# Reciprocal sums broadcast through a DRAM scratch, TensorE's steps from a table, border splits on VectorE

## The chip, the cores and the metric

One core of a Trainium2 chip runs one program in one launch. Time is in device microseconds. A core has TensorE (matmuls; PE in the profile, and PEld for its weight loads), VectorE (DVE), ScalarE (ACT), GpSimd (POOL), SyncE (SP, which here only issues transfers), and 16 DMA engines between DRAM and the on-chip memory. Each engine works through its own instructions in the order in which they were written for it; semaphores hold an instruction until what it needs is there.

## The reference, cut to what matters

Attention with a threshold, then two feed-forward layers. Scores that lie more than `tau` under their row's maximum are masked out; what is left is exponentiated and divided by its row sum.

```python
scores = (1 / np.sqrt(64)) * np.matmul(q, k.transpose(0, 1, 3, 2))   # 4 x 8 heads, 576 x 576
thresh = np.max(scores, axis=-1, keepdims=True) - tau
scores = np.where(scores >= thresh, scores, -1e9)
attn = np.exp(scores - np.max(scores, axis=-1, keepdims=True))
attn = attn / (np.sum(attn, axis=-1, keepdims=True) + 1e-09)
x = np.matmul(attn, v)                       # then to 2304 tokens x 512
h = x @ w_in                                 # 512 x 2048
x = (np.maximum(h, 0) + alpha * np.minimum(h, 0)) @ w_out
h = x @ w2_in
return (h * (1 / (1 + np.exp(-h)))) @ w2_out
```

## The kernel before

**Attention stage.** The 32 heads are worked in 16 pairs (`pairs`). A pair has nine units `t`: units 0 to 7 are 128 rows of queries of one head (even units the first head, odd ones the second), and unit 8 holds the last 64 rows of both heads. The steps of a unit, with the engine and the line of the profile:

- TensorE, `qkmm` (L345): scores of two units into PSUM, tile `s`.
- VectorE, `maxi` (L359): scales and negates the scores into a buffer `x` and takes the row's extreme.
- ScalarE, `expo` (L372) and `thr` (L379): the exponentials, tile `e` (unit 8: `z`), and the threshold.
- VectorE, `mask` (L385): multiplies the exponentials by the comparison with the threshold and takes the row sum into column 2 of `stat(i)`, tile `m`.
- TensorE, `trans` (L420): transposes the masked exponentials in pieces of 128 x 128 into a PSUM bank, tile `t`; ScalarE copies a bank into on-chip memory (`copy`, L130, tiles `pt`, `p`, `px`, `q`).
- TensorE, `pv` (L454, five steps per pair) and `pv8` (L461, unit 8): the product with the values.
- VectorE, `evac` (L468) and `evac8` (L475): bring the product into `X`, multiplied by the reciprocal of the row sum.

That product has queries along the free dimension, while the row sums stand one to a partition, so the reciprocals have to be turned. Before, this went by way of TensorE: `recip` (L394, three times per pair: four, four and one column), `spread` (L400, on ScalarE: each column copied 64 times into a tile `rb`), `transr` (L426: five more transposes per pair, into the same PSUM banks as transposes of the last key block), and the copies of those banks, which are twice as wide for it. `evac` and `evac8` then read the turned reciprocals from `px` and `q`.

**What sets the order.** TensorE's steps were one cycle, `CYCLE`, repeated for every pair with offsets (`Q2:-1` is the scores of unit 2 of the pair before). `plan` places every other engine's instructions: at each moment an engine takes, of what is ready by the planner's own durations, that with the lowest priority number. Idle TensorE time early on is filled with dummy matmuls on a zero tile (`idle`, L288: `WU` = 9 before all else, `WF` = 32 more where the planner sees a gap). The order so found is written out and kept by the engines. SyncE's queue holds the loads of `raw` (queries and keys), `rv` (values) and `wraw` (weights), in that order too.

**Weights and border.** The feed-forward layers take their weights split into a high and a low part (`wconv`, L164 to L180: about ten instructions per 128 x 512 piece, on ScalarE, VectorE and, after the attention stage, GpSimd: L176, L178). The eight pieces of the first quarter of the first layer are made during the attention stage, at low priority. The first product of the first layer, `mm_h` (L209), for tokens 0 to 511 is 48 matmuls into tiles `s`; `act1` (L218, L219) applies the activation and `hilo` (L130, L126) splits the result `g` into a high part (ScalarE) and a low part (VectorE); `ymm` (L625, L641) multiplies by the second weights, tile `y`. `xsplit` (L197) does the same splitting for `X`, with the low part on GpSimd (L126 on POOL, tile `xs`). From there on the layers are one long row of `h` and `y` matmuls. "The border" below is the stretch in which the attention stage ends and this row begins.

Of the kernel before, what the change touches and what calls it, by code (L numbers as in the profile page):

```python
# [36 lines left out]
WF = 32  # L37
# [8 lines left out]
CYCLE = (  # L46
# [56 lines left out]
def attn_moe_moe(  # L103
# [139 lines left out]
    with ExitStack() as pa:  # L243
# [7 lines left out]
        rbp = ent(name="rbp", bufs=2)  # L251
# [137 lines left out]
        def cols(ch):  # L389
            return (0, 1) if ch == 2 else (4 * ch + 1, 4 * ch + 5)  # L390

        def recip(i, ch):
            a, z = cols(ch)
            V.reciprocal(stat(i)[:, 2, a:z], stat(i)[:, 2, a:z])  # L394

        def spread(i, ch):
            a, z = cols(ch)
            n = 2 if ch == 2 else 4
            RS[i, ch] = rbp.tile([128, 4, 64], F32, tag="rb", name="rb")
            A.activation(out=RS[i, ch][:, :n], in_=stat(i)[:, 2, a:z].unsqueeze(2).to_broadcast([128, n, 64]), func=AF.Copy)  # L400

        cycle = [(x.split(":")[0], int(x.split(":")[1])) for x in CYCLE.split()]
        line = [(x, i + o) for i in range(0, NP + 2) for x, o in cycle if 0 <= i + o < NP]
# [45 lines left out]
        def pv(i, kt):  # L449
            if kt == 0:  # L450
                AV[i] = psV.tile([128, 512], F32, tag="pv", name="pv")
            for h in range(2):
                src = PT[i, "pt"][:, h, kt] if kt < KT - 1 else PT[i, "px"][:, 0]
                T.matmul(AV[i][h * 64:(h + 1) * 64], RV[i][:, h, kt], src, start=kt == 0, stop=kt == KT - 1)  # L454

        def pv8(i):
# [263 lines left out]
```

## Time and profile before

| what | value |
|---|---|
| median of 3 runs | 1078.13 us (1077.79 to 1078.48) |
| the profiled execution: time, span | 1078.86 us, 1077.1 us |
| mean granted TensorE clock | 0.997 |
| busy in the span: PE, PEld, DVE, ACT, POOL | 1067.9, 835.3, 745.3, 606.3, 357.4 us |
| attention stage (to the first of the 48 `h` matmuls) | 0 to 279.5 us |
| the 48 `h` matmuls, then the first 24 `y` matmuls | 279.5 to 290.6, to 296.2 us |
| TensorE idle, then at half clock | 296.2 to 298.8, about 300.0 to 303.4 us |
| rest of the layers | to 1077.1 us |

Busy time is the share of time in which an engine has an instruction in work; where one starts before the last has ended (VectorE's do), starts give the real spacing. In the chain of waits each moment belongs to the instruction that held up the end. A matmul's end is modelled, so the spacing of starts is used for TensorE too. The profiled execution's span is 1.76 us shorter than its time, and its time is 0.73 us above the median of the runs.

### The profile page before, as it was taken

The numbers are of one execution on the slowest core, as the hardware profiler recorded it, in microseconds if no ns is written. First come the engines' busy times: TensorE is split into PE (matmuls) and PEld (weight loads), VectorE is DVE, ScalarE is ACT, GpSimd is POOL, SyncE is SP. The second block draws the span as 40 slices with busy tenths as digits, with TensorE's granted clock in tenths as the row PEclk, the third lists the DMA queues.
The fourth block names the chain that finished last, engine by engine and source line by source line (L and its number), as shares of the span: only waits on it lengthen the run. The fifth ranks groups of instructions, "written<-read, shape, count | busy, mean of one in ns | idle before, by whom it ended". The sixth has DMA issues, their size and how long they took to land.

```text
span 1077.1 us, 15422 instructions
## 1 busy us (share of the span) xinstructions
PE 1067.9 (99%) x5749; PEld 835.3 (78%) x5749; DVE 745.3 (69%) x1403; ACT 606.3 (56%) x1177; POOL 357.4 (33%) x271
## 2 busy tenths in 40 slices
PE   9999999999999999999999999999999999999998
PEld 5656666566678888888888888888888888888887
DVE  7999999999766278558846864863478468543343
ACT  5898898888665455345534543565455354433321
POOL 0000000000355285256625742851566256323110
PEclk9999999999999999999999999999999999999999
DMA  3223232221222011101201110121012011000112
GB/s 107 74 92 96 70 104 66 81 84 39 79 79 79 1 59 59 40 19 60 79 1 40 59 59 1 59 64 35 19 61 79 1 40 59 1 1 1 40 59 79
DMA packets 19402, 57.09 MB, mean 53 GB/s; under 512 B 2432, under 2 KB 2816, under 8 KB 19328
## 3 DMA queue, kind: packets, MB, share of 16 engines
q1 hardware_dynamic: 18880, 55.71, 16.2%
q8 instruction: 45, 0.74, 0.3%
q10 hardware_dynamic: 448, 0.41, 0.1%
q14 instruction: 29, 0.24, 0.1%
HBM read 51.39 MB, written 4.72 MB: 52 GB/s over the span
## 4 chain that ended last, share of the span: by engine, by line
PE 94%; DVE 3%; ACT 1%; issue 1%; DMA 0%; POOL 0%; DVEq 0%; ACTq 0%; SPq 0%
PE h L209 36%; PE y L641 18%; PE y L625 18%; PE s L345 8%; PE t L420 6%; PE pv L454 6%; DVE x L359 1%; PE pv L288 1%; DVE e L385 1%; PE t L461 1%; PE t L426 1%; DMA wraw<-in_w1i 0%; ACT pt L130 0%; DVE wa L168 0%; DVE wm L166 0%
## 5 line engine op out<-in xcount | busy, mean ns | idle before, releaser
L209 PE MATMUL h<-xs,w 128*128 128x512 f32 (+1 forms) x1872 | 418.7, 368 | 0.0
L209 PEld LDWEIGHTS h<-xs,w 128*128 128x128 f32 x1872 | 329.8, 189 | 60.1
L176 POOL TENSOR_TENSOR wa<-wa,w 128x512 f32<-128x512 f32 x56 | 72.9, 1302 | 458.8 <-ACT w L172 359.9
L625 PE MATMUL y<-g,w 128*128 128x512 f32 (+1 forms) x960 | 216.9, 370 | 2.7 <-ACT g L130 2.7
L641 PE MATMUL y<-w,g 128*128 128x512 f32 x876 | 213.9, 387 | 0.0
L625 PEld LDWEIGHTS y<-g,w 128*128 128x128 f32 x960 | 169.9, 189 | 34.1 <-ACT g L130 3.1
L641 PEld LDWEIGHTS y<-w,g 128*128 128x128 f32 x876 | 161.4, 188 | 32.0
L126 DVE TENSOR_TENSOR g<-r,g 128x512 fp32r<-128x512 f32 (+1 forms) x160 | 140.0, 875 | 56.3 <-ACT g L130 54.9
L126 POOL TENSOR_TENSOR xs<-acc,xs 128x512 fp32r<-128x512 f32 (+1 forms) x80 | 106.0, 1355 | 133.5 <-ACT xs L130 133.4
L130 ACT ACTIVATE g<-r 128x512 fp32r<-128x512 f32 (+1 forms) x160 | 93.9, 587 | 92.5 <-DVE r L229 47.1
L126 POOL TENSOR_TENSOR xs<-X,xs 128x512 fp32r<-128x512 f32 (+1 forms) x72 | 98.7, 1399 | 57.5 <-ACT xs L130 57.1
L359 DVE TENSOR_SCALAR_CACHE_REDUCE x<-s,nsc 128x576 f32<-128x576 f32 x144 | 112.4, 814 | 7.1 <-PE s L345 6.1
L229 DVE TENSOR_TENSOR r<-h,r 128x512 f32<-128x512 f32 (+1 forms) x80 | 50.7, 634 | 92.7 <-ACT r L228 92.4
L219 DVE SCALAR_TENSOR_TENSOR r<-r,neg,h 128x512 f32<-128x512 f32 (+1 forms) x76 | 52.2, 686 | 73.8 <-ACT r L218 73.6
L345 PE MATMUL s<-raw 64*128 64x288 f32 (+1 forms) x576 | 100.6, 429 | 0.9 <-DVE x L359 0.9
L228 ACT ACTIVATE r<-h 128x512 f32<-128x512 f32 (+1 forms) x80 | 43.8, 547 | 102.2 <-PE h L209 101.7
L372 ACT ACTIVATE e<-x,m 128x576 f32<-128x576 f32 x128 | 97.0, 790 | 7.4 <-DVE x L359 7.4
L385 DVE SCALAR_TENSOR_TENSOR e<-x,m,e 128x577 f32<-128x577 f32 x128 | 99.7, 811 | 1.2 <-ACT m L379 1.0
L180 DVE TENSOR_TENSOR w<-we,wa 128x512 fp32r<-128x512 f32 x64 | 59.9, 935 | 46.1 <-POOL we L178 33.8
L345 PEld LDWEIGHTS s<-raw 64*128 64x128 f32 (+1 forms) x576 | 57.2, 188 | 40.8 <-DVE e L385 11.4
L172 ACT ACTIVATE w<-wa 128x512 fp32r<-128x512 f32 x64 | 40.7, 635 | 84.4 <-DVE wa L168 77.5
L178 POOL TENSOR_TENSOR we<-we,wm 128x512 f32<-128x512 f32 x56 | 81.6, 1457 | 18.2 <-ACT wm L174 18.2
(69 smaller groups left out, 1043.3 us busy)
## 6 DMA issues: line engine op xcount, KB each, us to landing
wraw<-in_w1i SPq DMA_DIRECT2D x16, 512.0 KB, 3.8
wraw<-in_w1o SPq DMA_DIRECT2D x16, 512.0 KB, 3.5
wraw<-in_w2i SPq DMA_DIRECT2D x16, 512.0 KB, 3.6
wraw<-in_w2o SPq DMA_DIRECT2D x16, 512.0 KB, 3.4
rv<-in_v SPq DMA_DIRECT2D x16, 480.0 KB, 3.5
raw<-in_q SPq DMA_DIRECT2D x15, 320.0 KB, 3.3
out<-o SPq DMA_DIRECT2D x17, 256.0 KB, 2.0
raw<-in_k SPq DMA_DIRECT2D x15, 288.0 KB, 2.8
```

Of the source, the lines that this page charges most:

```text
L126: le.tensor_tensor(out=lo, in0=src, in1=hi.bitcast(F32), op=ALU.subtract)
L130: e.activation(out=dst, in_=src, func=AF.Copy)
L176: e2.tensor_tensor(out=a, in0=a, in1=w[:, 0].bitcast(F32), op=ALU.subtract)
L178: e2.tensor_tensor(out=e, in0=e, in1=m, op=ALU.mult)
L209: nc.tensor.matmul(ps[:, :n], w[c][:, a, fl * 128:(fl + 1) * 128], xs[c][:, b, :n], start=k == 0, stop=k == 3 * NC - 1,)
L345: T.matmul(SP[u + k][:, hf, :S // 2], RAW[i][p, 0, q], RAW[i][p, 1, c], start=True, stop=True)
L359: V.tensor_scalar(out=x.rearrange("p (a b) -> p a b", a=2), in0=SP[u][:, :, :S // 2], scalar1=nsc, scalar2=None, op0=ALU.mult, op1=ALU.min ...
L372: A.activation(out=ES[u], in_=xts[u % XB][:, 1:S + 1], func=AF.Exp, bias=mcol(u, 0), scale=-1.0)
L385: V.scalar_tensor_tensor(out=e, in0=x, scalar=mcol(u, 1), in1=e, op0=ALU.is_le, op1=ALU.mult, accum_out=mcol(u, 2))
L420: T.transpose(TP[n][:, c * 128:(c + 1) * 128], EP[i, t // 2][:, o:o + 128], ident)
L625: nc.tensor.matmul(ys[e][:, :n], w[NC + fl][:, a, e * 128:(e + 1) * 128], gt[:, c, :n], start=fl == 0 and k == 0, stop=fl == G - 1 and k == 2,
L641: nc.tensor.matmul(y, gt[:, a, s * 128:(s + 1) * 128], w[NC + fl][:, c, cs], start=fl == 0 and k == 0, stop=fl == G - 1 and k == 2,)
```

## The change

- The reciprocals are taken once per pair, nine columns at a time (`recip`), then written to a DRAM scratch by one transfer that turns them (`keep`: 1152 elements of 4 bytes), and read back by four transfers that repeat them over 64 partitions each (`fetch`), into a tile `inv` in the layout that `evac` and `evac8` multiply by. `spread` and `transr` and their shares of the copies are gone; `evac8` is one instruction instead of two.
- TensorE's steps come from a table, `ORDER`, that gives each step of each pair its place, and priorities by kind (`PRIO`) replace those in the calls. `WF` goes from 32 to 16, and the first `pv` waits for the last filler.
- The first two weight pieces of the second quarter, and the split of `X` for tokens 1024 to 1535, have their low parts made by VectorE instead of GpSimd.

```diff
-WF = 32
+WF = 16
-CYCLE = (
-    "Q2:-1 T6:-2 T2:-2 T7:-2 T0:-2 Tr1:-2 Q4:-1 T8:-2 Rr1:-2 "
...
+ORDER = (
+    "Q0:0 Q2:0 T1:0 Q4:0 Q6:0 Tr0:0 T0:0 T3:0 Q8:0 T4:0 T2:0 Q0:1 T6:0 T7:0 T5:0 Q2:1 P0:0 Tr1:0 Q4:1 T8:0 T0:1 "
...
+PRIO = {'exp': 2, 'copy': -1, 'thr': 0.5, 'mask': 2.5, 'max': 0, 'recip': 2.5, 'evac': 0, 'evac8': 0, 'w': 2.5, 'xh': 2.5, 'xl': 2.5}
...
-            it = wconv(stage, pools[j // NC], wi, wo, g, j, nc.gpsimd)
+            it = wconv(stage, pools[j // NC], wi, wo, g, j, V if wi is w1i and g == 1 and j < 2 else nc.gpsimd)
...
-        def recip(i, ch):
-            a, z = cols(ch)
-            V.reciprocal(stat(i)[:, 2, a:z], stat(i)[:, 2, a:z])
-
-        def spread(i, ch):
...
+        def recip(i):
+            V.reciprocal(stat(i)[:, 2], stat(i)[:, 2])
+
+        def keep(i):
+            SC[i] = dram.tile([9, 128], F32, tag="inv", name="inv")
+            nc.sync.dma_start(SC[i].rearrange("t q -> q t"), stat(i)[:, 2])
+
+        def fetch(i):
+            RS[i] = ptp.tile([128, S], F32, tag="inv", name="inv")
+            for h in range(2):
+                src = SC[i][1:].rearrange("(j h) q -> h j q", h=2)[h].unsqueeze(0).to_broadcast([64, 4, 128])
+                nc.sync.dma_start(RS[i][h * 64:(h + 1) * 64, :512].rearrange("p (j q) -> p j q", q=128), src)
+            for h in range(2):
+                src = SC[i][0:1, h * 64:(h + 1) * 64].to_broadcast([64, 64])
+                nc.sync.dma_start(RS[i][h * 64:(h + 1) * 64, 512:], src)
...
-        def transr(n):
...
-            V.tensor_tensor(out=X[:, hp, b * S:b * S + 512], in0=AV[i], in1=PT[i, "px"][:, 1], op=ALU.mult)
+            V.tensor_tensor(out=X[:, hp, b * S:b * S + 512], in0=AV[i], in1=RS[i][:, :512], op=ALU.mult)
...
-            for h in range(2):
-                p = slice(h * 64, (h + 1) * 64)
-                V.tensor_tensor(
-                    out=X[p, hp, c0:c0 + 64], in0=TP[bank[i, "r8"]][p, 256:320],
-                    in1=PT[i, "q8"][p, 128 + h * 64:192 + h * 64], op=ALU.mult,
-                )
+            V.tensor_tensor(
+                out=X[:, hp, c0:c0 + 64], in0=TP[bank[i, "r8"]][:, 128:192], in1=RS[i][:, 512:], op=ALU.mult
+            )
...
+                op(("recip", i), "DVE", 0.16, 0, [("mask", pos[i, x]) for x in range(9)], lambda i=i: recip(i), 0.3)
+                op(("keep", i), "SP", 0.6, 1, [("recip", i), ("fetch", i - 2)], lambda i=i: keep(i), 5.0)
+                op(("fetch", i), "SP", 2.4, 1, [("keep", i), ("evac", i - 2), ("evac8", i - 2)], lambda i=i: fetch(i), 4.5)
...
-                xs = xsplit(X[:, :, t0:t0 + n] if m == 1 else ACC[t0 // 512], n, nc.scalar, nc.gpsimd)
+                le = V if (m, g, t0) == (1, 0, 1024) else nc.gpsimd
+                xs = xsplit(X[:, :, t0:t0 + n] if m == 1 else ACC[t0 // 512], n, nc.scalar, le)
```

TensorE, in the middle of the attention stage; `t<-ident` are transposes, of which those that read `rb` are the turned reciprocals. Before:

```order
L345 MATMUL s<-raw 128x288 x4
L420 MATMUL t<-ident,e 128x128 x12
L345 MATMUL s<-raw 128x288 x2
L420 MATMUL t<-ident,z 128x128
L420 MATMUL t<-ident,e 128x128 x6
L426 MATMUL t<-ident,rb 128x128 x3
L345 MATMUL s<-raw 128x288 x4
L454 MATMUL pv<-pt,rv 64x512 x2
```

and in the changed kernel:

```order
L464 MATMUL pv<-pt,rv 64x512 x6
L363 MATMUL s<-raw 128x288 x4
L436 MATMUL t<-ident,e 128x128 x2
L436 MATMUL t<-ident,z 128x128 x4
L436 MATMUL t<-ident,e 128x128 x8
L363 MATMUL s<-raw 128x288 x2
L436 MATMUL t<-ident,e 128x128 x4
L436 MATMUL t<-ident,z 128x128
```

The transposes of `rb` are gone, and the blocks between the score groups are mixed otherwise. Counting every change between scores, transposes and `pv` work as one, TensorE's row has 150 blocks before and 160 now (fillers and the first `h` matmuls counted with the transposes). Twelve of the 48 `h` matmuls now stand ahead of the last pair's `pv` steps; before, all 48 stood behind them. Of the sixteen fillers all now stand ahead of the fourth group of scores of the first pair.

SyncE's queue, a stretch in the middle of the attention stage. Before:

```order
L316 DMA raw_1869<-in_q 128x640
L332 DMA rv_1929<-in_v 128x960
L316 DMA raw_2045<-in_k 128x576
L316 DMA raw_2045<-in_q 128x640
L332 DMA rv_2113<-in_v 128x960
L158 DMA wraw_2123<-in_w1o 128x1024
L316 DMA raw_2235<-in_k 128x576
```

and now (`inv<-m` is `keep`, `inv<-inv` is `fetch`):

```order
L334 DMA raw_1772<-in_k 128x576
L334 DMA raw_1772<-in_q 128x640
L412 DMA inv_1829<-m_1634 128x9x1
L350 DMA rv_1832<-in_v 128x960
L418 DMA inv_1882<-inv_1829 64x4x128 x2
L421 DMA inv_1882<-inv_1829 64x64 x2
L176 DMA wraw_1907<-in_w1o 128x1024
L334 DMA raw_1949<-in_k 128x576
L334 DMA raw_1949<-in_q 128x640
```

Five issues per pair join the queue; for the last pair a `wraw` load stands between `keep` and `fetch`. On VectorE, between a pair's reciprocal and the first instruction that reads its `inv`, stand 17 to 24 other instructions for pairs 0 to 14, and 13 for the last.

VectorE at the border, from the first activation of the first layer on (`r`, then `g`; `wm`, `wa`, `we`, `w` belong to weight pieces). Before:

```order
L219 SCALAR_TENSOR_TENSOR r_3173<-r_3173,neg_76,s_3075 128x512
L126 TENSOR_TENSOR g_3174<-r_3173,g_3174 128x512
L219 SCALAR_TENSOR_TENSOR r_3179<-r_3179,neg_76,s_3075 128x512
L180 TENSOR_TENSOR w_3214<-we_3213,wa_3212 128x512
L126 TENSOR_TENSOR g_3180<-r_3179,g_3180 128x512
L166 TENSOR_SCALAR wm_3226<-wm_3226 128x512
L168 SCALAR_TENSOR_TENSOR wa_3227<-wraw_3224,wm_3226 128x512
L170 TENSOR_SCALAR we_3228<-wa_3227 128x512
L219 SCALAR_TENSOR_TENSOR r_3185<-r_3185,neg_76,s_3108 128x512
L126 TENSOR_TENSOR g_3186<-r_3185,g_3186 128x512
L219 SCALAR_TENSOR_TENSOR r_3191<-r_3191,neg_76,s_3108 128x512
L126 TENSOR_TENSOR g_3192<-r_3191,g_3192 128x512
```

and now:

```order
L237 SCALAR_TENSOR_TENSOR r_3044<-r_3044,neg_76,s_2803 128x512
L198 TENSOR_TENSOR w_2940<-we_2939,wa_2938 128x512
L144 TENSOR_TENSOR g_3045<-r_3044,g_3045 128x512
L237 SCALAR_TENSOR_TENSOR r_3050<-r_3050,neg_76,s_2803 128x512
L144 TENSOR_TENSOR xs_3336<-X_81,xs_3336 128x512
L144 TENSOR_TENSOR g_3051<-r_3050,g_3051 128x512
L144 TENSOR_TENSOR xs_3339<-X_81,xs_3339 128x512
L144 TENSOR_TENSOR xs_3342<-X_81,xs_3342 128x512
L184 TENSOR_SCALAR wm_3082<-wm_3082 128x512
L237 SCALAR_TENSOR_TENSOR r_3056<-r_3056,neg_76,s_2974 128x512
L186 SCALAR_TENSOR_TENSOR wa_3083<-wraw_3080,wm_3082 128x512
L144 TENSOR_TENSOR xs_3345<-X_81,xs_3345 128x512
```

The four `xs` splits and, further on, `wa` and `we` of two weight pieces come into VectorE's row and leave GpSimd's.

## Rows read from the trace of the kernel before

**Rows 1.** The page's first part: busy time, share of the span and number of instructions of each engine.

```profile
PE 1067.9 (99%) x5749; PEld 835.3 (78%) x5749; DVE 745.3 (69%) x1403; ACT 606.3 (56%) x1177; POOL 357.4 (33%) x271
```

**Rows 2.** Busy time of each engine in stretches of the run: from and to (us), length, then busy time and number of instructions of PE, PEld, DVE, ACT and POOL, the granted TensorE clock (1.00 is 2.4 GHz, 0.50 is 1.2 GHz), the DMA engines' share and GB/s.

```profile
28.85:176.63 147.78, 147.78 (x1101) 92.43 (x1102) 144.77 (x405) 130.21 (x275) 0.00 (x0) 1.00 0.28 87
176.63:211.16 34.53, 33.89 (x247) 21.10 (x248) 34.24 (x95) 31.23 (x67) 0.00 (x0) 1.00 0.27 81
...
290.55:296.20 5.65, 5.60 (x25) 4.32 (x23) 5.62 (x4) 2.57 (x5) 5.57 (x4) 1.00 0.04 14
296.20:298.80 2.60, 0.00 (x0) 0.00 (x1) 1.87 (x4) 1.80 (x4) 1.25 (x2) 1.00 0.00 0
298.80:303.11 4.31, 4.31 (x13) 3.38 (x13) 3.58 (x6) 1.64 (x3) 1.94 (x2) 0.64 0.40 122
...
320.00:1077.10 757.10, 752.92 (x3600) 634.38 (x3598) 452.30 (x625) 344.24 (x637) 335.37 (x250) 1.00 0.13 42
```

**Rows 3.** The chain of waits in order of time: start, length, what.

```profile
61.80 2.73 PE pv L454 x12
...
78.19 2.73 PE pv L454 x12
...
176.63 2.73 PE pv L454 x12
...
183.83 1.47 DVE e L385 x3
...
211.16 2.73 PE pv L454 x12
...
311.62 2.72 PE y L625 x12
```

**Rows 4.** Timeline of TensorE in the middle of the attention stage, transposes of `rb` only: start, length, engine, line, what.

```profile
227.29 0.38 PE L426 MATMUL t<-ident,rb 128*128 128x128 f32 x2
...
234.66 0.49 PE L426 MATMUL t<-ident,rb 128*128 128x128 f32 x3
```

**Rows 5.** Groups of instructions by line over the attention stage: busy time in us, mean ns of one, then idle time of the engine before them.

```profile
L426 PE MATMUL t<-ident,rb 128*128 128x128 f32 x80 | 14.1, 273 | 0.0
...
L394 DVE RECIPROCAL m<-m 128x4 f32<-128x4 f32 (+1 forms) x48 | 8.0, 166 | 0.0
L475 DVE TENSOR_TENSOR X<-t,q 64x64 f32<-64x64 f32 x32 | 6.8, 212 | 0.7 <-PE t L461 0.5
```

**Rows 6.** Timeline of VectorE around the end of a pair: start, length, engine, line, what.

```profile
236.35 0.82 DVE L359 TENSOR_SCALAR_CACHE_REDUCE x<-s,nsc 128x576 f32<-128x576 f32 x1
...
237.09 0.82 DVE L359 TENSOR_SCALAR_CACHE_REDUCE x<-s,nsc 128x576 f32<-128x576 f32 x1
...
237.83 0.18 DVE L394 RECIPROCAL m<-m 128x4 f32<-128x4 f32 x1
237.92 0.79 DVE L385 SCALAR_TENSOR_TENSOR z<-x,m,z 128x577 f32<-128x577 f32 x1
...
238.64 0.45 DVE L475 TENSOR_TENSOR X<-t,q 64x64 f32<-64x64 f32 x2
...
239.12 0.69 DVE L468 TENSOR_TENSOR X<-pv,px 128x512 f32<-128x512 f32 x1
239.73 0.15 DVE L394 RECIPROCAL m<-m 128x1 f32<-128x1 f32 x1
239.80 0.80 DVE L385 SCALAR_TENSOR_TENSOR e<-x,m,e 128x577 f32<-128x577 f32 x1
```

**Rows 7.** Timeline of VectorE and TensorE at the start and the end of the attention stage; in square brackets the idle time before, and who ended it.

```profile
7.05 0.82 DVE L359 TENSOR_SCALAR_CACHE_REDUCE x<-s,nsc 128x576 f32<-128x576 f32 x1 [1.28 <-PE s L345]
...
28.15 0.82 DVE L359 TENSOR_SCALAR_CACHE_REDUCE x<-s,nsc 128x576 f32<-128x576 f32 x1 [0.87 <-PE s L345]
...
26.88 1.24 PE L345 MATMUL s<-raw 64*128 64x288 f32 x8
...
279.53 11.18 PE L209 MATMUL s<-xs,w 128*128 128x512 f32 x48
```

**Rows 8.** Timeline of the border: VectorE, GpSimd and TensorE.

```profile
288.40 0.78 DVE L126 TENSOR_TENSOR g<-r,g 128x512 fp32r<-128x512 f32 x1 [0.70 <-ACT g L130]
...
290.30 6.12 POOL L126 TENSOR_TENSOR xs<-X,xs 128x512 fp32r<-128x512 f32 x4
...
292.07 1.78 DVE L126 TENSOR_TENSOR g<-r,g 128x512 fp32r<-128x512 f32 x1
...
295.31 1.66 DVE L168 SCALAR_TENSOR_TENSOR wa<-wraw,wm 128x512 int32<-128x512 int32 x1
...
298.80 4.51 PE L625 MATMUL y<-g,w 128*128 128x512 f32 x12 [2.65 <-ACT g L130]
```

**Rows 9.** Transfers by line: queue, number, size of each, median us from issue to landing.

```profile
rv<-in_v SPq DMA_DIRECT2D x16, 480.0 KB, 3.5
...
out<-o SPq DMA_DIRECT2D x17, 256.0 KB, 2.0
...
sc<-in_tau ACTq DMA_DIRECT2D x1, 0.5 KB, 4.0
```

**Rows 10.** Timeline of the issuing of two of them: start, and how long the issuing engine was at it.

```profile
1.36 0.84 ACTq L324 DMA_DIRECT2D sc<-in_tau  x1
...
234.09 0.33 SPq L316 DMA_DIRECT2D raw<-in_k  x1
```

More of the change, by code (lines that the diff above doesn't have):

```diff
@@ L250, in attn_moe_moe @@
         sm = ent(name="sm", bufs=4)
-        rbp = ent(name="rbp", bufs=2)
+        dram = ent(name="dram", bufs=2, space=bass.MemoryType.DRAM)
         stage = ent(name="stage", bufs=1)
@@ L293, in op @@
         def op(name, eng, dur, prio, deps, fn, fin=None):
-            ops[name] = (eng, dur, dur + 0.2 if fin is None else fin, prio, deps, fn)
-        KS, RV, RAW, HI, SP, ES, EP, MS, TP, PT, AV, RS = ({} for _ in range(12))
+            ops[name] = (eng, dur, dur + 0.2 if fin is None else fin, PRIO.get(name[0], prio), deps, fn)
+        KS, RV, RAW, HI, SP, ES, EP, MS, TP, PT, AV, RS, SC = ({} for _ in range(13))
         def dma(name, prio, deps, out, src, f=None):
@@ L387, in mask @@
             )
-        def cols(ch):
-            return (0, 1) if ch == 2 else (4 * ch + 1, 4 * ch + 5)
-        def recip(i, ch):
-            a, z = cols(ch)
-            V.reciprocal(stat(i)[:, 2, a:z], stat(i)[:, 2, a:z])
-        def spread(i, ch):
[L397 to L403, printed above, removed]
+        def recip(i):
[11 more added lines that the diff above has]
+                nc.sync.dma_start(RS[i][h * 64:(h + 1) * 64, 512:], src)
+        line = [(x.split(":")[0], int(x.split(":")[1])) for x in ORDER.split()]
         banks = []
@@ L511, in attn_moe_moe @@
                 op(("qk", u), "PE", 0.972 if t == 8 else 1.077, 0, ([("ld", i, 0), ("ld", i, 1)] if u else [("ld8",)]) + [("max", u + x - 2) for x in range(n)], lambda u=u: qkmm(u), 1.17 if t == 8 else 1.28)
-            op(("max", u), "DVE", 0.74, -1, [qk(u), ("tauv",), ("mask", u - XB), ("exp", u - XB)] + [("spread", i - 4, ch) for ch in range(3)], lambda u=u: maxi(u), 0.86)
+            op(("max", u), "DVE", 0.74, -1, [qk(u), ("tauv",), ("mask", u - XB), ("exp", u - XB)] + [("keep", i - 4)], lambda u=u: maxi(u), 0.86)
             if t == 8:
@@ L534, in attn_moe_moe @@
             order["t", n] = ("t", n - 1)
-            done, w = [("t", n)], len(g)
-            if kind in RCH:
-                op(("tr", n), "PE", 0.109 * len(g), 1, [("spread", i, RCH[kind])] + done, lambda n=n: transr(n), 0.109 * len(g) + 0.25)
-                order["tr", n] = ("t", n)
-                done.append(("tr", n))
-                w *= 2
-            free = {"8": [("pv8", i - 2)], "r8": [("evac8", i - 2)], "r0": [("evac", i - 2)]}.get(kind, [("pv", i - 2, KT - 1)])
-            op(("copy", n), "ACT", 0.08 + 0.1 * w, 0, done + free, lambda n=n: copy(n), 0.24 + 0.1 * w)
+            free = {"8": [("pv8", i - 2)], "r8": [("evac8", i - 2)], "r0": [("pv", i - 2, KT - 1)], "r1": [("pv", i - 2, KT - 1)]}.get(kind, [("pv", i - 2, KT - 1)])
+            op(("copy", n), "ACT", 0.08 + 0.1 * len(g), 0, [("t", n)] + free, lambda n=n: copy(n), 0.24 + 0.1 * len(g))
         for i in range(NP):
             op(("pv8", i), "PE", 0.637, 2, [("copy", bank[i, "8"]), ("copy", bank[i, "r8"]), ("v", i)], lambda i=i: pv8(i), 0.86)
-            op(("evac8", i), "DVE", 0.48, 0.5, [("pv8", i)], lambda i=i: evac8(i), 0.62)
+            op(("evac8", i), "DVE", 0.2, 0.5, [("pv8", i), ("fetch", i)], lambda i=i: evac8(i), 0.34)
             for kt in range(KT):
-                need = [("copy", bank[i, t]) for t in range(8)] + [("v", i), ("evac", i - 1)] if kt == 0 else [("pv", i, kt - 1)]
+                need = [("copy", bank[i, t]) for t in range(8)] + [("v", i), ("evac", i - 1), ("z", WF - 1)] if kt == 0 else [("pv", i, kt - 1)]
                 need += [("copy", bank[i, "r0"]), ("copy", bank[i, "r1"])] if kt == KT - 1 else []
@@ L550, in attn_moe_moe @@
                 order["pv", i, kt] = ("pv", i, kt - 1)
-            op(("evac", i), "DVE", 0.62, -1, [("pv", i, KT - 1)], lambda i=i: evac(i), 0.78)
+            op(("evac", i), "DVE", 0.62, -1, [("pv", i, KT - 1), ("fetch", i)], lambda i=i: evac(i), 0.78)
         WOPS = [("SP", 0.6)] + [("ACT", 0.52), ("DVE", 0.34), ("DVE", 0.61), ("DVE", 0.34), ("ACT", 0.52), ("ACT", 0.52), ("DVE", 0.61), ("DVE", 0.61), ("DVE", 0.61)]
@@ L589, in step @@
                 return "pv", i, int(a)
-            return "t" if k == "T" else "tr", bank[i, int(a) if a.isdigit() and a != "8" else a]
+            return "t", bank[i, int(a) if a.isdigit() and a != "8" else a]
         for k in range(WF):
```

30 lines of the change are left out of this document (9 added, 21 removed), and 21 rows, old and new, of tables (CYCLE, ORDER).

## The prediction

> **What bounds the kernel now.** I read the busy shares first: TensorE 99%, VectorE 69% [rows 1]. That average hides two regimes, so I cut the span into stretches [rows 2]. From 320 us to the end TensorE is busy 752.92 of 757.10 us while VectorE is at 60%: the layers are TensorE's, no edit touches their instruction order, and I move them as a block. In the attention stage, 28.85 to 176.63 us, TensorE is busy throughout and VectorE 144.77 of 147.78 us: two engines are full at once. The chain of waits says who leads: the same `pv` group comes back after 78.19 - 61.80 = 16.39 us [rows 3], and (176.63 - 28.85) / 9 = 16.42 us is the period of a pair [rows 2]; it is TensorE's steps that fill it. Only from 183.83 us does the chain pass to VectorE: two periods take 34.53 us instead of 32.84, so 1.7 us are lost there [rows 2, 3]. So neither engine's saving alone shortens a pair; the smaller of the two does. Last, the border: TensorE stands for 2.65 us before a block of 12 `y` matmuls, and these take 4.51 us, while the next such block takes 2.72 [rows 3, 8]. The granted clock in that stretch is 0.64, that is partly the lower level, 1.2 GHz [rows 2]. The border loses 2.65 + 1.79 = 4.4 us.
>
> Why TensorE stands there is in VectorE's row: a low part `g` takes 0.78 us, and 1.78 us while GpSimd's four `xs` splits run (290.30 to 296.42 us); `wa` takes 1.66 us in that time [rows 8]. VectorE is slowed by GpSimd's work and the `g` that TensorE waits for comes late.
>
> **TensorE's part in the attention stage.** Two transposes of `rb` hold 0.38 us of the timeline and three 0.49 [rows 4], so one more costs 0.11 us. Eighty of them go [rows 5]: -8.8 us. The new order has 160 blocks against 150; the first transpose of a block costs 0.38 - 0.11 - 0.11 = 0.16 us more than the others [rows 4]; I take 0.1 us for each of ten more changes: +1.0. Both lie on the path, since TensorE has no idle time there.
>
> At the start, the third score group of pair 1 begins at 26.88 us in the trace [rows 7]. In the new order VectorE has 22 passes over a unit's 576 columns (`maxi` or `mask`) and one reciprocal to do before that group has its two PSUM buffers; a pass starts 0.74 us after the one before [rows 6], the first at 7.05 us [rows 7]; with about 1.5 us of waits for the first exponentials, 7.05 + 22 x 0.74 + 0.1 + 1.5 = 24.9 us. That is 2.0 us sooner, and the `pv` step (a fourth of the 2.73 us that three of them hold with their change of mode [rows 3], 0.9 us) is already behind it: -2.9. Halving the fillers gives nothing by itself: fillers fill time in which TensorE would wait for VectorE anyway.
>
> The 1.7 us of 183 to 211 us should go too, as VectorE gets lighter. Against that, 12 of the 48 `h` matmuls now come before the last `pv`: 48 of them start at 279.53 [rows 7] and the `y` matmuls at 290.55 [rows 2], 11.0 us for 48, so 12 hold +2.7. With TensorE packed from the start, the last `pv` ends 8.8 - 1.0 + 2.9 + 1.7 - 2.7 = 9.7 us sooner.
>
> **VectorE's part.** The spacing in the trace: a pass 0.74, a reciprocal of four columns 0.09, of one 0.07, the two `evac8` 0.48, the `evac` 0.61 [rows 6]. Per pair 18 x 0.74 + 0.25 + 0.48 + 0.61 = 14.66 us, and what is left of 16.42 us, 1.8, goes to weight pieces and splits. Now: one reciprocal at 0.1, one `evac8` at half of 0.48. That saves 0.15 + 0.24 = 0.4 us a pair, 6.3 us in 16 pairs. TensorE's pair shrinks by 0.55 - 0.06, to 15.9 us, and VectorE's with its side work to 16.0. They are full within 1% of each other, so each will now and then wait for the other. I allow 1.6 us for it and take -8.1 at the last `pv`; the bounds are -10.6 (TensorE packed, and 0.9 us of gaps ahead of the last `pv` closed as well by the `h` matmuls) and -2.8 (VectorE's 6.3 only, and a tail after its last pass that is 3.5 us longer, since more transposes and `pv` steps are left there).
>
> ScalarE loses its spreads and part of its copying; it is busy 130 of 147.78 us [rows 2], so this is cover and counts nothing.
>
> **The border.** After the last `pv` 36 `h` matmuls remain instead of 48: -2.7. So the first `y` comes 10.8 us sooner. Then the four splits and four weight instructions go from GpSimd to VectorE: some 8 x 0.69 = 5.5 us more of its work (the length of `evac`, a like instruction [rows 6]), against 1.0 us of stretching at `g` and about as much at `wa` [rows 8] that it loses. Adding up its row in the new order from the last `evac` with these lengths, the three `g` come some 6, 8 and 13 us after the last `pv`; TensorE wants them at 8.2, 10.9 and 13.6. The gap closes, and with it the stretch at 1.2 GHz: -4.4, from -4.4 (all) to 0 (the third `g` has only half a microsecond to spare). For the last pair `fetch` stands behind a weight load on SP's queue, whose buffer ScalarE frees late; behind it on VectorE wait `evac8`, `evac` and all of the border's work: +0.5, from 0 to 4.
>
> **The DRAM round trip.** No such transfer is in the trace. SP spends 0.33 us on an issue of 128 rows and ScalarE's queue 0.84 us on 128 elements of 4 bytes [rows 10], which land after 4.0 us; 128 rows of values land in 3.5, the quickest transfer in 2.0 [rows 9]. So `keep`, nine times as many 4-byte elements, lands between 4.0 us and 2.0 + 9 x 2.0 = 20 us; I take 6, near the lower end, as those 4.0 us were spent beside the first loads of queries and keys. `fetch` has four issues and 640 short rows: 1.2 + 4 us. Round trip 11.2 us (8.5 to 26). It is hidden by the 17 to 24 VectorE instructions between the reciprocal and the first use, which last 12.2 to 16.4 us at the spacings of [rows 6], 14.1 in the mean. So it costs nothing; but the cover is thin, and `evac8` stands in VectorE's row with all score passes behind it. On SP the next loads of `raw` queue behind `fetch`; they are needed a whole pair later.
>
> **The sum**, against the profiled execution's own 1078.86 us: -8.1 - 2.7 - 4.4 + 0.5 = -14.7, so 1064.2; the median of the runs lies 0.73 lower, so 1063.5.
>
> **Rivals.**
> - *The round trip is not hidden* (slower). Above 12.2 us VectorE waits in pair after pair; at 16 us the shortfalls under the 16 covers sum to about 30 us. It eats the whole gain from 15 us on; at 16 us the time is 1063.5 + 30 = 1093. For: 1152 tiny elements, a wait on SP that no cover shows. Against: the 4.0 us for 128. Chance 0.07. The Trainium skill speaks against such a transfer: "DMA: Bandwidth & Descriptors", "Rules for kernel authors", has a non-contiguous last dimension become one descriptor per element and asks for it to be rearranged, and its "Measured" table, for transfers issued from GpSimd, puts the smallest at about 10.5 ns a packet, over a fixed part of about 2.0 us ("Anatomy of one DMA"). By those figures (an estimate) `keep` takes 14.1 us, `fetch` 8.7, and the time would be some 140 us longer, 1203; no run here shows it yet, and I give 0.02 of the 0.07 to it.
> - *VectorE binds* (-2.8 at the last `pv`, the border as forecast): -2.8 - 2.7 - 4.4 = -9.9, or 1068. For: the balance of 15.9 and 16.0. Against: its waits for TensorE, as the 0.87 us at 28.15 [rows 7], now have slack to vanish in. Chance 0.16.
> - *The border keeps its gap*: late `fetch`, or VectorE's fuller row delays the third `g`, and TensorE falls to 1.2 GHz again: -8.1 - 2.7 = -10.8 plus 1 for `fetch`, or 1068.5. Chance 0.10.
> - *TensorE runs at 1.2 GHz early on*, since half of the fillers are gone and it idles for short times between 13 and 24 us. The granted clock fell after 2.6 us of idleness [rows 2], and such gaps here are near 1 us. At half clock some 3 us more: 1066.5. Chance 0.04. The Trainium skill, "TensorE: Matmul & The Clock Gate", "Part 4: PE-mode transpose", says that transposes do not count as TensorE activity as other matmuls do, which would make this likelier; in 28.85 to 176.63 us, full of transposes, the clock is 1.00.
> - *It does nothing measurable*: hardly possible, with eighty instructions off a full engine. 0.02.
>
> **Chances and range.** Forecast 0.61. Faster by over 0.2% 0.91, within 0.2% (about what a measurement of this kernel can tell) 0.02, slower 0.07. The best that the bounds allow is -10.6 - 2.7 - 4.4 = -17.7, or 1060.5; with 2 us for what the spacings leave out the range begins at 1058.5. It ends at 1071, beyond the second and third rivals, and leaves out the first and parts of the edges.
>
> **What would show it.** `pv` groups repeating every 15.9 to 16.1 us; the last `pv` near 271.4 us; no VectorE wait named after an `inv` transfer; `g` near 0.78 us at the border, no gap of TensorE there and the clock at 1.00. Wrong would be: VectorE idle before L483 or L478 with `inv` as what ended it, `keep` landing after more than 8 us, or a gap with a lower clock at the first `y` blocks.

## The result and the profile after

| | before | after |
|---|---|---|
| median of the runs, us | 1078.22 (1077.79 to 1078.48) | 1087.18 (1085.55 to 1088.03) |
| ratio to before, 95% interval | | 1.0082 [1.0064, 1.0099] |
| profiled execution, us: time, span | 1078.86, 1077.1 | 1087.38, 1085.7 |

The kernel became 9.0 us slower where 14.7 us less was forecast. All the profile rows of this section are of the changed kernel. The page's first part answers to [rows 1]: TensorE and VectorE have less to do, and the span is longer all the same.

```profile
PE 1064.3 (98%) x5653; PEld 826.0 (76%) x5653; DVE 740.0 (68%) x1363; ACT 586.7 (54%) x1129; POOL 347.6 (32%) x263
```

By stretches (columns as in [rows 2]) the loss is in the attention stage: of the 31.15 us from 28.85 to 60, TensorE is busy for 26.62; before it had no idle time there.

```profile
28.85:60.00 31.15, 26.62 (x186) 15.53 (x185) 24.18 (x67) 18.87 (x41) 0.00 (x0) 0.95 0.50 95
282.00:306.00 24.00, 21.15 (x121) 14.76 (x120) 15.05 (x28) 11.06 (x22) 0.00 (x0) 1.00 0.45 95
306.00:345.00 39.00, 38.71 (x171) 31.49 (x170) 30.37 (x47) 24.46 (x45) 17.67 (x12) 1.00 0.26 82
```

The chain of waits (start, length, what) names transfers that the chain of before does not have. The block of 12 `y` that stood at 311.62 [rows 3] now stands at 320.15: the whole loss has been made by then.

```profile
24.68 1.18 PE s L363 x8
...
37.62 12.51 DMA wraw<-in_w1i
...
77.65 9.81 DMA inv<-m
89.50 2.64 DMA inv<-inv
96.19 8.98 DMA inv<-m
107.20 3.37 DMA inv<-inv
...
320.15 2.72 PE y L625 x12
```

Its shares by line up to 345 us say that most of what it holds in transfers is the round trip itself: `keep` 23.4%, `fetch` 7.3%, the weight load 3.6%.

```profile
by line: DMA inv<-m 23.4%; PE s L363 11.6%; PE t L436 8.7%; DMA inv<-inv 7.3%; PE pv L464 6.2%; PE h L227 5.7%; issue 5.4%; DVE x L377 5.0%; PE y L625 4.6%; DMA wraw<-in_w1i 3.6%; DVE e L403 3.1%; SPq L418 2.7%; SPq L421 1.6%; DMA raw<-in_q
```

The transfers by line (number, size of each, median us to landing; [rows 9] has `rv` of before at 3.5): `keep` is `inv<-m`, at 9.6 us, and the value loads have become slower, though nothing about them was edited.

```profile
rv<-in_v SPq DMA_DIRECT2D x16, 480.0 KB, 6.6
...
inv<-inv SPq DMA_DIRECT2D x32, 128.0 KB, 3.4
inv<-inv SPq DMA_DIRECT2D x32, 16.0 KB, 2.9
inv<-m SPq DMA_DIRECT2D x16, 4.5 KB, 9.6
```

SP's timeline (start, length) shows how. A weight load is issued 0.42 us behind `keep` and lands 12.5 us later (the chain); then SP stands until `keep` has landed, spends 2.5 us on the four issues of `fetch`, and only then issues the loads of `raw`.

```profile
37.20 0.38 SPq L412 DMA_DIRECT2D inv<-m  x1
37.62 1.76 SPq L176 DMA_DIRECT2D wraw<-in_w1i  x1
39.48 0.38 SPq L350 DMA_DIRECT2D rv<-in_v  x1
48.72 1.27 SPq L418 DMA_DIRECT2D inv<-inv  x2
50.03 1.24 SPq L421 DMA_DIRECT2D inv<-inv  x2
51.38 0.53 SPq L334 DMA_DIRECT2D raw<-in_k  x1
```

The other engines at that place (idle time in square brackets, with who ended it): ScalarE stands before `wm`, the first step on the weight piece. Behind `wm` in its row are the thresholds that VectorE's masks need and the copies that free TensorE's banks, so all three engines stand.

```profile
50.15 0.66 ACT L182 ACTIVATE wm<-wraw 128x512 f32<-128x512 f32 x1 [6.34 <-DMA wraw<-in_w1i]
51.69 0.82 DVE L403 SCALAR_TENSOR_TENSOR e<-x,m,e 128x577 f32<-128x577 f32 x1 [4.45 <-ACT m L397]
52.85 1.12 PE L436 MATMUL t<-ident,e 128*128 128x128 f32 x4 [4.53 <-ACT pt L148]
```

The list of waits up to 345 us (total, times, longest) has both ways in which the round trip reaches the compute engines: VectorE before its evictions, 12.1 us in seven places, and ScalarE before weights, 18.6 us in five.

```profile
ACT wm L182 <- DMA wraw<-in_w1o: 10.6, 3, 6.6
...
DVE X L483 <- DMA inv<-inv: 10.2, 6, 2.2
...
ACT wm L182 <- DMA wraw<-in_w1i: 8.0, 2, 6.3
...
DVE X L478 <- DMA inv<-inv: 1.9, 1, 1.9
```

The border went as foreseen. Its timeline answers to [rows 8]: `g` at 0.69 us instead of 1.78, gaps of 0.77 and 0.29 us instead of 2.65 ahead of the `y` blocks, and the granted clock 1.00 in the stretches above. TensorE first:

```profile
302.76 6.83 PE L625 MATMUL y<-g,w 128*128 128x512 f32 x28 [0.77 <-ACT g L148]
...
309.88 2.11 PE L625 MATMUL y<-g,w 128*128 128x512 f32 x8 [0.29 <-DVE g L144]
```

VectorE's timeline beside it:

```profile
304.79 0.69 DVE L144 TENSOR_TENSOR g<-r,g 128x512 fp32r<-128x512 f32 x1
```

### The profile page after: what moved, and what is told of

Its sections match the earlier page's. It is cut to its first block, busy times and chain, and to the rows that moved or that the text cites. A ratio compares the mean times of both kernels' runs of the same rounds, so it can differ in the third digit from the quotient of the medians.

```text
span 1085.7 us, 15296 instructions
## 1 busy us (share of the span) xinstructions
PE 1064.3 (98%) x5653; PEld 826.0 (76%) x5653; DVE 740.0 (68%) x1363; ACT 586.7 (54%) x1129; POOL 347.6 (32%) x263
## 2 busy tenths in 40 slices
DMA packets 49354, 61.88 MB, mean 57 GB/s; under 512 B 24192, under 2 KB 32768, under 8 KB 49280
## 4 chain that ended last, share of the span: by engine, by line
PE 80%; DMA 11%; DVE 5%; issue 2%; SPq 1%; ACT 1%; DVEq 0%
PE h L227 35%; PE y L641 18%; PE y L625 18%; DMA inv<-m 7%; PE s L363 4%; PE t L436 3%; DMA inv<-inv 2%; PE pv L464 2%; DVE x L377 2%; DMA wraw<-in_w1i 1%; DVE e L403 1%; SPq L418 1%; SPq L421 1%; DMA raw<-in_q 0%; DVE X L478 0%
## 5 line engine op out<-in xcount | busy, mean ns | idle before, releaser
L194 POOL TENSOR_TENSOR wa<-wa,w 128x512 f32<-128x512 f32 x54 | 70.4, 1304 | 485.0 <-DVE we L188 354.5
L363 PE MATMUL s<-raw 64*128 64x288 f32 (+1 forms) x576 | 105.1, 432 | 3.7 <-DVE x L377 3.5
L144 POOL TENSOR_TENSOR xs<-X,xs 128x512 fp32r<-128x512 f32 (+1 forms) x68 | 93.2, 1400 | 48.6 <-ACT xs L148 48.3
L436 PEld LDWEIGHTS t<-ident,e 128*128 128x128 f32 x576 | 64.0, 142 | 38.9 <-issue 14.6
L436 PE MATMUL t<-ident,e 128*128 128x128 f32 x576 | 80.6, 281 | 10.8 <-ACT pt L148 6.6
```

What stands on the lines that cost most here:

```text
L144: le.tensor_tensor(out=lo, in0=src, in1=hi.bitcast(F32), op=ALU.subtract)
L194: e2.tensor_tensor(out=a, in0=a, in1=w[:, 0].bitcast(F32), op=ALU.subtract)
L363: T.matmul(SP[u + k][:, hf, :S // 2], RAW[i][p, 0, q], RAW[i][p, 1, c], start=True, stop=True)
L436: T.transpose(TP[n][:, c * 128:(c + 1) * 128], EP[i, t // 2][:, o:o + 128], ident)
```

## The experiments

Each time stands with its ratio to runs of the kernel before on the same chip (medians there 1077.5 to 1078.1 us).

### Is the round trip the whole loss?

**No transfers.** `keep` and `fetch` stay in the plan as empty steps, so that every other instruction keeps its place.

```diff
         def keep(i):
+            pass
...
         def fetch(i):
+            pass
...
-            V.tensor_tensor(out=X[...], in0=AV[i], in1=RS[i][:, :512], op=ALU.mult)
+            V.tensor_tensor(out=X[...], in0=AV[i], in1=ones[:, :512], op=ALU.mult)
```

> The changed kernel with the same instruction order, but without `keep` and `fetch`: the evictions multiply by a tile of ones, so the attention output is left unnormalised. Theory A (the DRAM round trip is the whole loss: 9.6 us to land the 1152 elements, four issues of 0.6 us, 2.6 us of landing, 14.7 us against a cover of 14.1, and what queues behind it on SP): the forecast without its 0.5 us for the late fetch, 1063, within 2 us; pv period near 16.0 us. Theory B (TensorE's new order and VectorE's balance are themselves slower than taken): 1075 or more, with VectorE and TensorE still waiting for one another in the attention stage.

Measured 1060.98 us, 0.984 [0.9827, 0.9853], 2.0 us under theory A's 1063, at the edge of what it allowed. Theory B falls. From 20 us to the end of the last `pv` TensorE has no idle time (busy time by stretches of this run):

```profile
20.00:269.00 249.00, 249.00 (x1822) 151.05 (x1819) 242.87 (x642) 206.16 (x429) 0.00 (x0) 1.00 0.25 80
```

TensorE's timeline of the same run has the end of the last `pv`, 267.94 + 1.03 = 268.97, and the border without a gap:

```profile
267.94 1.03 PE L459 MATMUL pv<-px,rv 128*64 128x512 f32 x4
277.21 8.32 PE L620 MATMUL y<-g,w 128*128 128x512 f32 x36
285.37 8.32 PE L227 MATMUL h<-xs,w 128*128 128x512 f32 x36
293.53 2.88 PE L620 MATMUL y<-g,w 128*128 128x512 f32 x12
```

**Transfers that nobody reads.** `keep` and `fetch` as in the changed kernel, evictions with ones.

> `keep` and `fetch` run as in the changed kernel, but the evictions multiply by a tile of ones, so nothing on VectorE waits for the round trip; the output is unnormalised. Theory A1 (VectorE's waits for `inv`, 12.1 us in seven places, are the loss): as without transfers, about 1064. Theory A2 (what stands behind `keep` and `fetch` on SP's queue, above all the weight load that took 12.5 us at 37.62 us and value loads at 6.6 instead of 3.5 us, is a large part): 1070 to 1076, with ScalarE's wm still waiting 5 us or more for wraw. Theory B: 1080 or more.

Measured 1085.43 us (1081.48 to 1088.76), 1.0064 [1.0047, 1.008]: nearly the whole loss, without one wait for `inv`. Theory A1 falls. The number lies where theory B had put it, but the run without transfers has ruled that theory out. A2 had the right place and too small a size: ScalarE's waits for weights have grown to 25.9 us (this run's list of waits from 20 to 310 us):

```profile
ACT wm L182 <- DMA wraw<-in_w1o: 16.7, 3, 6.2
...
ACT wm L182 <- DMA wraw<-in_w1i: 9.2, 3, 5.6
```

Value loads now land after 9.4 us (transfers by line):

```profile
rv<-in_v SPq DMA_DIRECT2D x16, 480.0 KB, 9.4
```

### What makes it dear: the elements

**Rows of 36 bytes.**

```diff
-            SC[i] = dram.tile([9, 128], ...)
-            nc.sync.dma_start(SC[i].rearrange("t q -> q t"), stat(i)[:, 2])
+            rows = dram.tile([128, 9], ...)
+            nc.sync.dma_start(rows, stat(i)[:, 2])
+            SC[i] = rows.rearrange("q t -> (q t)").rearrange("(t q) -> t q", q=128)
```

> `keep` writes 128 rows of 36 bytes, as the tile lies, instead of 1152 single elements; `fetch` is unchanged, so the inverses reach the wrong queries. Theory A (the 1152 elements are what makes `keep` slow): it lands in 2.5 to 4 us, the round trip is 8 us, under the smallest cover of 12.2, no VectorE wait after an `inv` transfer, and the time is 1063 to 1066. Rival (a write to DRAM with its completion takes that long whatever its shape): `keep` still lands after 8 us or more and the time stays at 1087.

Measured 1060.98 us, 0.984 [0.9827, 0.9853], the time without any transfer. The same bytes go out and come back; only the number of pieces has changed, and `keep` lands in 2.3 us (transfers by line). The pages count the pieces: the changed kernel moves 24192 packets under 512 B, this run 7808; the 16384 fewer are what 16 `keep`s of 1152 - 128 pieces less each would make.

```profile
rv<-in_v SPq DMA_DIRECT2D x16, 480.0 KB, 3.8
...
inv<-m SPq DMA_DIRECT2D x16, 4.5 KB, 2.3
```

**Pieces of 12 bytes.** The same with `rows` as [3, 128, 3]: 384 pieces.

> `keep` writes 384 pieces of 12 bytes (three columns at a time), which reach `fetch` in the wrong order. With 128 pieces in 2.3 us and 1152 in 9.6, 7.1 ns a piece: 4.1 us to land, a round trip of 9.3 us, below the smallest cover of 12.2: 1061 to 1066. If the cost went by bytes or were a step of its own for pieces under some size: about 9 us to land and 1080 or more.

Measured 1061.11 us, 0.9847 [0.9834, 0.9861]; `keep` lands in 3.8 us, where 4.1 had been worked out. So 128, 384 and 1152 pieces take 2.3, 3.8 and 9.6 us, and the first two cost the kernel nothing.

### By which way it reaches the time

**`keep` alone, unread.** `fetch` is an empty step, the evictions multiply by ones.

> `keep` alone on SP's queue, no `fetch`, evictions by ones (unnormalised). SP no longer stands still until `keep` has landed; loads are issued on time but land behind the elements of `keep` on the same queue. If the loss comes from SP standing (loads issued 9 us late): 1061 to 1065. If it comes from the loads' place behind the elements in the queue: wraw and rv issued within 2 us of `keep` still take 8 us or more, and the time is 1072 to 1086.

Measured 1072.64 us, 0.9959 [0.9945, 0.9973]: 11.7 more than without transfers, the second of the two expectations: SP no longer stands, and the loads still land late. Two weight loads behind the elements stand in this run's chain of waits; the median of such a load is 3.4 to 3.9 us in the changed kernel. So the elements on the loads' own queue cost 11.7 us; the next run shows that not all of it needs the same queue. The unread `fetch`, with SP's standing before it, brings the 12.8 more of the run above.

```profile
38.29 13.75 DMA wraw<-in_w1i
...
272.62 9.53 DMA wraw<-in_w1o
```

**From GpSimd's queue, unread.** In `keep` and `fetch` `nc.gpsimd.dma_start` replaces `nc.sync.dma_start`, in the plan "POOL" replaces "SP"; the evictions multiply by ones.

> `keep` with its 1152 elements and `fetch` run from GpSimd's DMA queue and nobody reads what they bring (evictions multiply by ones; output unnormalised). Both ways into the time are cut: VectorE's wait for `inv` and the loads' place behind `keep`. If these two are all, 1061 to 1064. If the elements also slow the other queue's transfers by filling the DMA engines: 1068 or more, with value and query loads over 5 us.

Measured 1067.87 us, 0.991 [0.9896, 0.9923], between the two readings: 6.9 more than without transfers. The loads are alone on SP's queue and still take 6 us (transfers by line; 3.5 and 3.3 without transfers).

```profile
rv<-in_v SPq DMA_DIRECT2D x16, 480.0 KB, 6.1
raw<-in_q SPq DMA_DIRECT2D x15, 320.0 KB, 6.2
```

These slower loads cost nothing before the end: TensorE is busy for 250.00 of the 250 us from 20 to 270. What is lost goes by one weight load, issued on SP's queue at 265.10 while the last pair's elements are written from the other one (260.69 to 270.91). ScalarE waits 10.0 us for it (list of waits), and TensorE's only gaps, 5.4 us in all, stand at the first `y` blocks behind it. With the elements on SP's queue the load at this place took 9.5 us (272.62 in the run above), so that part of the cost does not come from sharing a queue.

```profile
ACT wm L182 <- DMA wraw<-in_w1o: 10.6, 2, 10.0
```

**From GpSimd's queue, read.** The same queue, evictions with the real inverses.

> `keep` (1152 single elements) and `fetch` are issued from GpSimd's DMA queue, which is idle in the attention stage; SP keeps the loads. Theory Q (the loads wait because they stand behind `keep` and `fetch` on one queue): weight and value loads land again in 3.5 to 5 us, and the time falls to 1061 to 1070, the upper end if VectorE still waits for `inv`. Theory D (the elements fill the DMA engines that all queues share): value loads still take 6 us or more and the time stays above 1078. Theory R (the length of the round trip is what counts, by VectorE's own wait): `inv` waits of 12 us or more remain and the time stays above 1078, though the loads are quick.

Measured 1130.67 us, 1.0482 [1.0465, 1.0499]. Theory R's waits are there, though the loads are not as quick as it had them (value loads 4.9 us). Against the unread run of the same queue the reading alone costs 62.8 us: TensorE's idle time grows by 37.0 us and its busy time by 25.8, as the granted clock from 20 to 345 us is 0.92 here and 1.00 there. From reciprocal to eviction 16 to 20 us pass in this run (81.56 to 98.04, 101.73 to 121.53), and VectorE's list of waits from 20 to 310 us has 45 us for L483 (57.6 in the whole run):

```profile
DVE X L483 <- DMA inv<-inv: 45.0, 11, 7.4
```

**Weight loads from GpSimd's queue.**

```diff
-    def wconv(stage, pool, wi, wo, g, j, e2):
+    def wconv(stage, pool, wi, wo, g, j, e2, q=nc.sync):
...
-        nc.sync.dma_start(raw, wsrc(...))
+        q.dma_start(raw, wsrc(...))
...
-            it = wconv(stage, (wpa, wpo)[j // NC], w1i, w1o, 0, j, V)
+            it = wconv(stage, (wpa, wpo)[j // NC], w1i, w1o, 0, j, V, P)
```

> Only the eight weight loads of the attention stage leave SP's queue for GpSimd's; keep, fetch, raw and rv stay. Theory Q with the weight loads as the main carriers of the loss (ScalarE waited 18.6 us for wraw, holding the copies that free TensorE's banks): ScalarE's waits for wraw go, 1068 to 1074. If the value and query loads or VectorE's waits for `inv` carry it: 1080 or more. Theory D: no change, 1085 to 1088, wraw still late.

Measured 1089.91 us (1086.22 to 1093.94), 1.0113 [1.0095, 1.0131]: no gain. ScalarE's waits for weights fall to 9 us, but the loads land after 8 us there too, and VectorE's waits for `inv` grow from 12.1 to 29.2 us, 28.3 of them at L483. Where one wait goes, the other takes its place.

```profile
DVE X L483 <- DMA inv<-inv: 28.3, 9, 9.2
```

**Planned with the measured durations.**

```diff
-  op(("keep", i), "SP", 0.6, 1, [...], lambda i=i: keep(i), 5.0)
-  op(("fetch", i), "SP", 2.4, 1, [...], lambda i=i: fetch(i), 4.5)
+  op(("keep", i), "SP", 0.6, 1, [...], lambda i=i: keep(i), 10.0)
+  op(("fetch", i), "SP", 2.4, 1, [...], lambda i=i: fetch(i), 5.5)
```

> The planner is told the measured durations (keep 10.0 us to land instead of 5.0, fetch 5.5 instead of 4.5), so that it puts the evictions and the loads later in the rows of VectorE, ScalarE and SP; TensorE's table stays. If VectorE's waits for `inv` at badly placed evictions were a cause of their own, they go and the time falls by some 10 us, to 1077. By theory Q, with the loads still behind `keep`, it stays within 1080 to 1090.

Measured 1118.14 us (1110.04 to 1121.94), 1.036 [1.0327, 1.0393], far outside both. The planner used SP's longer standing: four weight loads now go out within half a microsecond behind a `keep` (one does in the changed kernel), and each takes about 13 us (this run's chain of waits). That was not foreseen, and it is the plainest dose of the queue's cost. A better duration in the plan made the kernel slower: nothing in the plan prices a place behind `keep`.

```profile
37.85 12.86 DMA wraw<-in_w1i
96.97 13.58 DMA wraw<-in_w1i
...
164.88 12.95 DMA wraw<-in_w1o
...
300.70 12.83 DMA wraw<-in_w1o
```

### The border alone, and versions without the elements

**The kernel before with the border's splits on VectorE.** The last two hunks of the change (lines 204 and 660), nothing else.

> The kernel before with only the border's part of the change (four xs splits and two weight pieces on VectorE). By the prediction's border step: 4.4 us less, 1073.8, no gap ahead of the first y blocks and the granted clock at 1.00 there. Rival (VectorE's fuller row delays the third g): between 1076 and 1079, a gap of TensorE over 1 us stays.

Measured 1074.75 us, 0.997 [0.9958, 0.9981]: 3.4 less. Between the first `y` (289.74) and the block of 12 behind the next `h` (306.68) 16.94 us pass, against 290.55 to 311.46, 20.91, in the kernel before: 4.0 us at the border itself. One short gap is left.

```profile
296.57 2.11 PE L625 MATMUL y<-g,w 128*128 128x512 f32 x8 [0.28 <-DVE g L126]
```

**Rows by TensorE.**

```diff
                 T.transpose(TP[n][:, c * 128:(c + 1) * 128], EP[i, t // 2][:, o:o + 128], ident)
+            if kind == "r1":
+                T.transpose(TP[n][:9, 256:384], stat(i)[:, 2], ident)
...
-            nc.sync.dma_start(SC[i].rearrange("t q -> q t"), stat(i)[:, 2])
+            nc.sync.dma_start(SC[i], PT[i, "row"])
```

> The changed kernel, but TensorE turns the nine columns of inverses into nine rows (one transpose of 128x9 per pair in the half-empty bank of Tr1, one ScalarE copy), and `keep` writes 9 rows of 512 bytes; the whole computation is done. Theory (single elements were the cost): `keep` lands in 2 to 3 us; 16 more transposes at 0.11 to 0.4 us; so 1061.0 of the run with 36-byte rows plus 2 to 6 us, 1063 to 1067. Rival (a later start of the round trip, since the rows wait for Tr1 and its copy, makes VectorE wait for `inv`): 1070 or more, with waits named after `inv`.

Measured 1085.15 us, 1.0069 [1.0056, 1.0082]. The transfer is quick (`fetch` is issued 1.3 to 3 us behind `keep`), and VectorE waits for `inv` once, for 0.7 us, so neither reading holds. `Tr1` now needs the reciprocal, and in seven pairs TensorE reaches it first: 13.1 us of TensorE's own idle time (list of waits). The run stands 24.2 us above the one with 36-byte rows; the granted clock, 0.77 from 45 to 60 us (0.52 from 53.5, behind a gap of 2.81 us), is part of the rest, and what else is in it was not followed up.

```profile
PE t L438 <- DVE m L408: 13.1, 7, 2.8
```

**Rows by VectorE.**

```diff
-            V.reciprocal(stat(i)[:, 2], stat(i)[:, 2])
+            V.reciprocal(inv[i % 2][:, :9], stat(i)[:, 2])
+            RW[i] = sm.tile([128, 32], F32, tag="row", name="row")
+            V.transpose(out=RW[i], in_=inv[i % 2])
...
-            SC[i] = dram.tile([9, 128], ...)
-            nc.sync.dma_start(SC[i].rearrange("t q -> q t"), stat(i)[:, 2])
+            SC[i] = dram.tile([32, 128], ...)
+            nc.sync.dma_start(SC[i].rearrange("t (b q) -> b t q", b=4), RW[i])
```

> The changed kernel, whole computation, with one more VectorE instruction per pair: it turns the reciprocals in blocks of 32 by 32, so that `keep` writes 128 runs of 128 bytes straight into the rows that `fetch` reads. Theory (only the single elements were dear): `keep` lands in 2 to 3 us as with 36-byte rows, 16 instructions of 0.1 to 0.2 us are added, 1061 to 1065, and so ahead of both kernels. Rival (like the version with rows by TensorE, a further step between reciprocal and eviction opens a new wait): 1072 or more.

Measured 1064.02 us, 0.9873 [0.986, 0.9887]: the whole computation, 13.5 us faster than the kernel before and 23 faster than the changed one. `keep` now writes 128 runs of 128 bytes. The 16 added instructions hold 3.4 us (groups of instructions), which fits the 3.0 us by which it stands above the run with 36-byte rows.

```profile
L414 DVE STREAM_TRANSPOSE row<-inv 128x32 f32<-128x32 f32 x16 | 3.4, 211 | 0.6
```

## Why the prediction was wrong, step by step

- **TensorE's and VectorE's part: right in kind, 2.5 us too small.** -8.1 at the last `pv` was forecast, with -10.6 as the bound for a packed TensorE. Without transfers the last `pv` ends at 268.97 against 279.60: -10.6. The 1.6 us allowed for waits between the two engines did not come, and the 0.9 us of gaps closed. TensorE is busy throughout and VectorE for 242.87 of 249 us, so the rival *VectorE binds* falls, and the granted clock of 1.00 from 12 to 269 us answers the rival of a low clock early on. The `pv` groups come back every (200.49 - 57.21) / 9 = 15.9 us, as forecast. The start is right to 0.2 us: the third score group of pair 1 begins at 24.68 (forecast 24.9).
- **The border: right.** -4.4 forecast; -4.6 without transfers (first `y` to the block of 12: 293.53 - 277.21 = 16.32 against 20.91), -3.7 in the changed kernel, -4.0 with the border alone. That GpSimd's work had slowed VectorE is borne out by `g` at 0.69 us with that work moved.
- **All but the round trip** gives 1060.98 - 1078.14 = -17.2, where the prediction's terms without `fetch` make -15.2.
- **The failed step is "So it costs nothing"**, in the part on the DRAM round trip. The round trip was put at nothing there, and at +0.5 for the last pair at the border; it cost 1087.18 - 1060.98 = +26.2. Both signs that the prediction had named for this came: `keep` landing after more than 8 us, and VectorE idle before L483 and L478 for `inv`. Two things in the step were wrong. The term was mis-sized: `keep` takes 9.6 us, not 6, SP spends 2.5 us on the issues of `fetch`, not 1.2, and the round trip in the chain is 89.50 + 2.64 - 77.65 = 14.5 us, not 11.2. That is past the mean cover of 14.1, and VectorE waits for 12.1 us. (The bounds given there, 8.5 to 26, do not follow from its terms: 4.0 + 5.2 and 20 + 5.2 make 9.2 to 25.2. It changes nothing here.) And the mechanism was incomplete: the prediction asked only whether the result comes in time for VectorE. It named what queues behind `fetch` on SP, found `raw`, which has a pair's time in hand, and stopped. It did not look for the weight and value loads, nor for what stands in ScalarE's row behind `wm`.
- **What took its place**, from runs that add one thing at a time: elements written and nothing else +11.7; `fetch` and SP's standing +12.8; VectorE's wait for the result +1.8 (1087.18 - 1085.43, not clear of the noise, as the two intervals overlap). The parts hold in this order only, because the two ways into the time stand in for each other. With nobody reading, ScalarE's waits for weights grow from 18.6 to 25.9 us; with the weights on another queue, VectorE's waits for `inv` grow from 12.1 to 29.2; with the elements on another queue than the loads, the same reading costs 62.8 us. So the first rival was right that the round trip isn't hidden. The place it gave, VectorE's wait, is real, and the chain of waits goes through it; but it is not the only one, and taking it away alone brings back 1.8 us of 26.2.
- **How it reaches TensorE.** The profiled executions lie 1085.7 - 1059.1 = 26.6 us apart. TensorE's idle time makes 15.0 of that (21.4 against 6.4) and its longer busy time 11.6 (1064.3 against 1052.7). Part of the second is the granted clock, which is 0.89 from 45 to 60 us, behind the gap of 4.53 us, and 0.90 from 225 to 240, so partly the lower level, 1.2 GHz: 0.11 x 15 + 0.10 x 15, some 3 us (an estimate from these figures). What the rest is stays open.
- **The rule weighed in the prediction.** The rows show 1152 pieces in 9.6 us and 128 in 2.3, on the same queue. The Trainium skill, "DMA: Bandwidth & Descriptors", "Rules for kernel authors", was right that such a transfer becomes one descriptor per element and is to be rearranged; the packets counted above agree. With its per-packet price, measured on another queue, the estimate of 14.1 us was too long, and the forecast of 1203 far off. The same page of the Trainium skill, "Queues, rings and completion order", says that each DMA engine takes descriptors in the order of its ring; the weight loads of 12 to 14 us right behind `keep` agree. Its section "Issuing engines are not separate DMA queues" has transfers of all issuing engines run on the same DMA engines; that agrees with value and query loads of 6 us beside elements from GpSimd's queue.

Two points stay open. How the 12.8 us divide between SP's standing and the 640 short rows of `fetch` was not tried apart; with quick `keep` the same `fetch` costs nothing. And which of the late loads costs how much is read from waits, not from runs that move one load at a time, save for the weights.

## What to carry to other kernels

Count a transfer in pieces, not in bytes, and ask of every new transfer three things: when its reader needs it, what is queued behind it on its queue, and what stands behind the waiters of those on their engines. A small strided write between two loads can cost more than the work that it saves, and it shows first in transfers that nobody edited. If a layout must be turned round on the way to DRAM, turn it on an engine that has a fraction of a microsecond to spare, and write whole runs; and remember that a planner which is told a longer wait will fill it with work that then sits in the wrong place.

## What was not expected of the hardware

- From 384 to 1152 pieces of a transfer on SP's queue, each costs (9.6 - 3.8) / 768 = 7.6 ns; from 128 to 384, (3.8 - 2.3) / 256 = 5.9 ns. The bytes were the same 4.5 KB.
- A load issued 0.4 us behind 1152 elements takes 12.5 to 13.8 us instead of 3.4 to 3.9, longer than the elements themselves (9.6 to 10.7).
- With the elements on GpSimd's queue, loads of queries on SP's queue still went from 3.3 to 6.2 us.
- VectorE turns 128x32 in blocks of 32 by 32 in 0.21 us.
